# Third tokens loaded from ScalarE's queue instead of SyncE's, the third root on ScalarE, and the fourth statistics in two halves

## The chip, the cores and the metric

The kernel runs on one core of a Trainium2 chip. Its engines are TensorE (PE: matmuls, with its weight loads shown as PEld), VectorE (DVE), ScalarE (ACT), GpSimd (POOL) and SyncE (SP), which here only issues transfers. The metric is the device time of one execution in microseconds (us); lower is better. Beside it stands the span of the profiled execution, from its first to its last instruction.

## What is computed

Two mixers of the same input x (2048 tokens by 512 features) are blended by a gate. A is a spectral filter: a 2-D Fourier transform, a product with complex weights, the inverse transform. B normalizes each token, then runs a two-layer network over the token axis.

```python
def reference(A_x, A_w_r, A_w_i, B_x, B_w1, B_b1, B_w2, B_b2, gate_w):
    def _A_ref(x, w_r, w_i):
        X = rfft2(x.astype(float32), axes=(-2, -1))
        return irfft2(X * (w_r + 1j * w_i), s=(2048, 512), axes=(-2, -1)).astype(bfloat16)

    def _B_ref(x, w1, b1, w2, b2):
        h = _layernorm(x, axis=-1)                      # (x - mean) / sqrt(var + 1e-5)
        u = _gelu(einsum("bsd,sf->bdf", h, w1) + b1)    # S = 2048 -> F = 1792
        y = einsum("bdf,fs->bds", u, w2) + b2           # F -> S
        return y.transpose(0, 2, 1)

    x = A_x
    g = sigmoid((x * gate_w).sum(-1, keepdims=True))
    return g * _A_ref(x, A_w_r, A_w_i) + (1 - g) * _B_ref(x, B_w1, B_b1, B_w2, B_b2)
```

Both mixers take A_x; B_x is not read.

## The kernel before

The 2048 tokens are 16 blocks b of 128. The tokens of blocks 0 to 7 lie in the tile xa, those of 8 to 15 in xb; `hn` holds the normalized tokens. `w1a` holds the first 1024 of the 1792 columns of w1, by token block. The first long loop of TensorE (`mm1`, L279) goes over the token blocks: for each b it makes eight matmuls of 128x512, one for each group of 128 columns (ft), all eight adding up in PSUM over the 16 blocks. A block's matmuls need `hn` of that block and its part of `w1a`. Before the loop, L244 makes matmuls on a tile of zeros, and L243 turns the row b1 into a column with a matmul into a PSUM bank `pb`; ScalarE copies that to `bcol` (L305). The eighth column group of the loop takes over the bank of `pb`, so block 0's eighth matmul waits for that copy.

All order is written out by hand: engines run their instructions in the order of the program's text, and each waits by semaphores for what it needs. A wait stops its engine's later instructions too. A transfer of SP or ScalarE raises a semaphore when it has landed. There are eight such semaphores for both queues, taken in rotation; a transfer whose semaphore was used before waits until the earlier one has landed.

SP issues the loads at the start (L118 to L146): tokens of block 0, w1a of block 0, tokens 1, tokens 2, w1a 1, tokens 3, w1a 2, tokens 4 and 5, w1a 3 and so on. ScalarE issues b1 (`brow`, L121) in between.

The normalization of a block takes these steps:

- `bstat` (L250): statistics of the block's tokens, on VectorE; then their aggregate, `bn_aggr`, to mean and variance in `mv`.
- Blocks 0 and 1 (L300 to L307): ScalarE takes the square root (L303), VectorE the reciprocal (L306) and the normalization `norm_dve` (L275).
- Blocks 2 to 5: `aggr` (L255) adds 1e-5 on VectorE (L259) and takes the power -0.5 on GpSimd (L262); then `norm_dve`. The next block's statistics stand between, in the time in which GpSimd works.
- From block 6 on the normalization is an instruction of ScalarE (L271).

After the second root ScalarE loads the table for Sine (L309) and makes the angles `ma` and `mc` (L311, L312) for the Fourier tables.

Later TensorE alternates between the stages of the spectral filter, `token` (L513: L522, L525, L526), `dpass` (L534), `inv_tok` (L660, L666) and `inv_d` (L682), and products of the network that are pulled in between as filling (`fill`: L467 for the rest of the first layer, L477 and L809 for the second). Where each stage stands among the filling is fixed by the text (`fill_to`). VectorE prepares the stages' operands: YA and YB (L413 to L446), PMA and PMB (L540 to L571), then the outputs. L457 on ScalarE empties the second layer's banks, L811 on VectorE its last one.

Of the kernel before, what the change touches and what calls it, by code (L numbers as in the profile page):

```python
# [12 lines left out]
F32 = mybir.dt.float32  # L13
I32 = mybir.dt.int32

P = 128
# [6 lines left out]
NDVE = 6  # L23
# [20 lines left out]
def kernel(  # L44
# [13 lines left out]
    nc = tc.nc  # L58
# [5 lines left out]
    small = ctx.enter_context(tc.tile_pool(name="small", bufs=1))  # L64
# [3 lines left out]
    def H(i, shape, name, dt=BF16):  # L68
        return big.tile(shape, dt, tag=f"h{i}", name=name)
# [11 lines left out]
    xv = A_x[0].rearrange("(b a) d -> a b d", a=P)  # L81
    w1v = B_w1.rearrange("(b a) f -> a b f", a=P)
    w2v = B_w2.rearrange("(ft f) s -> f ft s", f=P)
    xh = [H(0, [P, 8, D], "xa"), H(1, [P, 8, D], "xb")]
# [4 lines left out]
    def load_x(b0, b1):  # L89
        nc.sync.dma_start(out=xh[b0 // 8][:, b0 % 8:(b1 - 1) % 8 + 1], in_=xv[:, b0:b1])  # L90

    def load_w1a(b0, b1):
        nc.sync.dma_start(out=w1a[b0 // 4][:, b0 % 4:(b1 - 1) % 4 + 1], in_=w1v[:, b0:b1, 0:FT1 * P])
# [27 lines left out]
    nc.scalar.dma_start(out=brow[:], in_=B_b1.rearrange("(ft f) -> ft f", f=P))  # L121
    load_w1a(0, 1)
    load_x(1, 2)
    for b in range(1, 3):
        load_x(b + 1, b + 2)
        load_w1a(b, b + 1)
    load_x(4, 6)
    load_w1a(3, 4)
    load_x(6, 8)
# [101 lines left out]
    stats = small.tile([P, NB, nc.vector.BN_STATS_DIM], F32, name="stats")  # L231
    mv = small.tile([P, NB, nc.vector.BN_AGGR_DIM], F32, name="mv")
# [16 lines left out]
    def bstat(b):  # L249
        nc.vector.bn_stats(out=stats[:, b, :], in_=xh[b // 8][:, b % 8, :])  # L250

    def on_dve(b):
        return b <= NDVE or b == NB - 2

    def aggr(b0, b1):  # L255
        for b in range(b0, b1):
            nc.vector.bn_aggr(out=mv[:, b, :], in_=stats[:, b, :])
        eng = nc.vector if on_dve(b0) else nc.gpsimd
        eng.tensor_scalar(mv[:, b0:b1, 1], mv[:, b0:b1, 1], 1e-5, 0.0, op0=Alu.add, op1=Alu.add)  # L259
        if not on_dve(b0):  # L260
            nc.gpsimd.tensor_scalar(nmr[:, b0:b1], mv[:, b0:b1, 0], -1.0, 0.0, op0=Alu.mult, op1=Alu.add)
        nc.gpsimd.tensor_tensor(rstd[:, b0:b1], mv[:, b0:b1, 1], c_mhalf.to_broadcast([P, b1 - b0]), op=Alu.pow)  # L262
# [11 lines left out]
    def norm_dve(b):  # L274
        nc.vector.tensor_scalar(hn[:, b, :], xh[0][:, b, :], mv[:, b, 0:1], rstd[:, b:b + 1],  # L275
                                op0=Alu.subtract, op1=Alu.mult)
# [20 lines left out]

    bcol = small.tile([P, NFT + NB], F32, name="bcol")
    b1f, b2f = bcol[:, 0:NFT], bcol[:, NFT:]
    for b in range(2):  # L300
        bstat(b)
        nc.vector.bn_aggr(out=mv[:, b, :], in_=stats[:, b, :])
        nc.scalar.activation(rstd[:, b:b + 1], mv[:, b, 1:2], ActF.Sqrt, bias=consts[:, 5:6], scale=1.0)  # L303
        if b == 0:
            nc.scalar.copy(b1f, pb[:, 0:NFT])  # L305
        nc.vector.reciprocal(rstd[:, b:b + 1], rstd[:, b:b + 1])  # L306
        norm_dve(b)  # L307
    bstat(2)
    nc.scalar.activation(sink[:], consts[:, 2:3], ActF.Sin, bias=c_mpi, scale=0.0)  # L309
    for v in range(2):  # L310
        nc.scalar.activation(ma[v][:], krow[:], ActF.Identity, bias=consts[:, 3 + v:4 + v], scale=acol[:, 0:1])  # L311
    nc.scalar.activation(mc[:], acol[:, 0:1], ActF.Identity, bias=consts[:, 4:5], scale=1024.0)  # L312


    aggr(2, 3)
    for b in range(2, NDVE):
        bstat(b + 1)
        norm_dve(b)
        aggr(b + 1, b + 2)
    bstat(NDVE + 1)  # L320
    norm(NDVE, NDVE + 1)
    aggr(NDVE + 1, NDVE + 2)
    norm(NDVE + 1, NDVE + 2)
    for b in range(NDVE + 2, NB, 2):
# [16 lines left out]
    for q in range(4):  # L341
        gprod(q)
        if q == 0:
# [10 lines left out]
                                in_=TD[:].rearrange("p s t k -> p (s t k)"))  # L354
    nc.sync.dma_start_transpose(out=TB[:].rearrange("p s t k -> p (s t) k"),
                                in_=TA[:].rearrange("p s t k -> p (s t k)"))
# [447 lines left out]
    b = NB - 1  # L804
# [36 lines left out]
```

## Time and profile before

| | |
|---|---|
| time, median of 3 runs | 128.1 us (127.78 to 128.22) |
| the profiled execution's own time | 128.74 us |
| its span | 127.0 us |
| mean granted TensorE clock | 0.998 |
| busy: TensorE, VectorE, ScalarE, GpSimd | 96%, 88%, 71%, 31% |
| HBM read, written | 19.15 MB, 3.67 MB |
| mean DMA rate | 189 GB/s (360 to 385 GB/s between 9.5 and 22 us) |

The busy share of an engine is a mean over the span. In the page's rows a group's time is followed by its mean for one instruction and by the idle time of its engine just ahead of it, with what ended that. In the order of time a row has the start, the time taken, the engine, the line, the operation, and what it writes and reads; SPq and ACTq are the issues of transfers on SP's and ScalarE's queues, whose time is that of the issue alone, not of the transfer. Matmuls overlap: one takes 0.38 us from start to end, but they follow each other every 0.216 us.

### The profile page before, as it was taken

How to read it: one execution, taken by the hardware profiler on the slowest of the kernel's cores; microseconds unless marked ns; L12 is line 12 of the kernel's file. 1: busy time of each engine (PE TensorE's matmuls, PEld its weight loads, DVE VectorE, ACT ScalarE, POOL GpSimd, SP SyncE). 2: the span in 40 equal slices, each digit the busy share in tenths (PEclk: the TensorE clock that was granted, in tenths of full speed). 3: DMA queues.
4: the chain of work that ended last, by engine and by line, in shares of the span. 5: the costliest groups of instructions: out<-in, count | busy, mean ns of one | idle time of the engine just before them, and what ended most of it. 6: DMA issues, size and time to landing. Idle time of an engine off the chain costs nothing.

```text
span 127.0 us, 2067 instructions
## 1 busy us (share of the span) xinstructions
PE 121.9 (96%) x737; PEld 65.3 (51%) x750; DVE 111.4 (88%) x190; ACT 89.6 (71%) x137; POOL 39.7 (31%) x71
## 2 busy tenths in 40 slices
PE   6999999999999999999999999999999999999990
PEld 2244444444444577657764775467644444444480
DVE  3799999999999999999999999999889999992140
ACT  4391379999799789998995699229795599422420
POOL 7133687998864595000050000000000000251200
PEclk9999999999999999999999999999999999999999
DMA  3899999998999999999979305810012101279991
GB/s 108 239 316 385 372 362 360 294 251 253 304 113 230 216 292 295 289 289 289 267 200 298 88 0 153 264 43 0 0 52 64 53 5 46 78 91 195 172 218 31
DMA packets 34699, 24.05 MB, mean 189 GB/s; under 512 B 5600, under 2 KB 32096, under 8 KB 34688
## 3 DMA queue, kind: packets, MB, share of 16 engines
q1 hardware_dynamic: 32580, 21.02, 63.2%
q0 software_dynamic: 1936, 2.76, 11.9%
q8 instruction: 6, 0.10, 0.3%
q10 hardware_dynamic: 172, 0.13, 0.3%
q14 instruction: 5, 0.04, 0.1%
HBM read 19.15 MB, written 3.67 MB: 180 GB/s over the span
## 4 chain that ended last, share of the span: by engine, by line
PE 93%; DMA 2%; DVE 1%; issue 1%; ACT 0%
PE yb L477 35%; PE u L279 23%; PE u L467 16%; PE ivt L666 5%; PE ivd L682 3%; PE dp L534 3%; PE yb L809 2%; PE tok L526 2%; PE tok L525 2%; DMA xa<-in_A_x_dram 2%; DVE stats L250 1%; PE ivt L660 0%; PE tok L522 0%; DVE hn L275 0%; DVE tbv L811 0%
## 5 line engine op out<-in xcount | busy, mean ns | idle before, releaser
L477 PE MATMUL yb<-gl,w2t 128*128 128x512 bf16 x203 | 46.4, 379 | 0.4
L477 PEld LDWEIGHTS <-w2t 128*128 128x128 bf16 x210 | 20.2, 98 | 22.0
L279 PE MATMUL u<-hn,w1a 128*128 128x512 bf16 x126 | 28.7, 388 | 0.2
L467 PE MATMUL u<-hn,w1b 128*128 128x512 bf16 x92 | 22.6, 379 | 0.2
L457 ACT ACTIVATE tbv<-yb,ombb,omg 128x512 bf16<-128x512 f32 x15 | 11.6, 776 | 15.8 <-PE yb L477 15.8
L279 PEld LDWEIGHTS <-w1a 128*128 128x128 bf16 x128 | 12.7, 99 | 16.2 <-issue 2.0
L787 POOL DMA_DIRECT2D out_dram<-ap x3 | 4.0, 1530 | 48.9 <-DVE ap L782 44.8
L467 PEld LDWEIGHTS <-w1b 128*128 128x128 bf16 x96 | 9.0, 98 | 8.0
L290 ACT ACTIVATE junk<-prod 128x512 bf16<-128x512 bf16 x16 | 10.1, 632 | 0.3
L361 ACT ACTIVATE gl<-u,bcol 128x512 bf16<-128x512 f32 x14 | 9.1, 685 | 1.0 <-PE u L279 0.8
L638 ACT CAST R<-ivt 128x1024 bf16<-128x1024 f32 x8 | 7.8, 1040 | 2.3 <-PE ivt L666 2.3
L262 POOL TENSOR_TENSOR rstd<-mv,consts 128x1 f32<-128x1 f32 (+1 forms) x10 | 6.5, 652 | 7.5 <-DVE mv L259 7.5
L638 ACT CAST H<-ivd 128x1024 bf16<-128x1024 f32 x7 | 6.9, 1050 | 0.8 <-PE ivd L682 0.8
L271 ACT ACTIVATE hn<-xb,nmr,rstd 128x512 bf16<-128x512 bf16 x8 | 5.8, 801 | 0.9 <-POOL nmr L266 0.9
L796 DVE TENSOR_TENSOR tbv<-tbv,ap 128x512 bf16<-128x512 bf16 x3 | 1.3, 426 | 5.8 <-ACT tbv L457 5.8
L250 DVE BATCH_NORM_STATS2 stats<-xa 128x6 f32<-128x512 bf16 x8 | 5.5, 686 | 0.6 <-DMA xa<-in_A_x_dram 0.5
L556 DVE TENSOR_TENSOR tatb<-PMA,wn 128x1024 bf16<-128x1024 bf16 x8 | 5.0, 688 | 0.2 <-PE tok L526 0.2
L606 POOL TENSOR_SCALAR omg<-g__765 128x16 f32<-128x16 f32 x1 | 0.7, 704 | 14.1 <-ACT g__765 L604 14.1
L682 PEld LDWEIGHTS <-R 128*128 128x128 bf16 x64 | 3.8, 98 | 2.5 <-ACT R L638 2.5
L250 DVE BATCH_NORM_STATS2 stats<-xb 128x6 f32<-128x512 bf16 x8 | 5.1, 674 | 0.0
L556 DVE TENSOR_TENSOR tatb<-PMB,wn 128x2048 bf16<-128x2048 bf16 x4 | 4.7, 1226 | 0.2
L527 ACT CAST ZA<-tok 128x1024 bf16<-128x1024 f32 x4 | 4.0, 1018 | 1.4 <-PE tok L526 1.3
(198 smaller groups left out, 226.5 us busy)
## 6 DMA issues: line engine op xcount, KB each, us to landing
w2t<-in_B_w_dram SPq DMA_DIRECT2D x8, 896.0 KB, 9.6
w1b<-in_B_w_dram SPq DMA_DIRECT2D x3, 1024.0 KB
w1a<-in_B_w_dram SPq DMA_DIRECT2D x8, 256.0 KB, 5.2
out_dram<-tbv SPq DMA_DIRECT2D x14, 128.0 KB, 4.4
out_dram<-ap POOLq DMA_DIRECT2D x3, 512.0 KB, 6.9
w1a<-in_B_w_dram SPq DMA_DIRECT2D x2, 512.0 KB
w1a<-in_B_w_dram SPq DMA_DIRECT2D x1, 1024.0 KB
xa<-in_A_x_dram SPq DMA_DIRECT2D x4, 128.0 KB, 3.2
```

What stands on the lines that cost most here:

```text
L250: nc.vector.bn_stats(out=stats[:, b, :], in_=xh[b // 8][:, b % 8, :])
L262: nc.gpsimd.tensor_tensor(rstd[:, b0:b1], mv[:, b0:b1, 1], c_mhalf.to_broadcast([P, b1 - b0]), op=Alu.pow)
L279: nc.tensor.matmul(u1[ft], lhsT=w1a[b // 4][:, b % 4, ft * P:(ft + 1) * P], rhs=hn[:, b, :], start=(b == 0), stop=(b == NB - 1))
L290: nc.scalar.activation(junk[:], prod[b // 8][:, b % 8], ActF.Copy, accum_out=glog[:, b:b + 1])
L361: nc.scalar.activation(gl[:, ft, :], src, ActF.Gelu_apprx_tanh, bias=b1f[:, ft:ft + 1], scale=1.0)
L457: nc.scalar.activation(tbv[0][:, b], y[:], ActF.Identity, bias=gate["ombb2"][:, b:b + 1], scale=gate["omg"][:, b:b + 1])
L467: nc.tensor.matmul(u[:], lhsT=w1b[c][:, b, k * P:(k + 1) * P], rhs=hn[:, b, :], start=(b == 0), stop=(b == NB - 1))
L477: nc.tensor.matmul(y[:], lhsT=w2t[b // 2][:, ft, (b % 2) * P:(b % 2 + 1) * P], rhs=gl[:, ft, :], start=(ft == 0), stop=(ft == NFT - 1))
L556: mul(tt[:, i, :, r:r + n], PM[:, 2 * s:2 * s + 2, r:r + n], w[:, None].to_broadcast([P, 2, n, 256]))
L638: nc.scalar.copy(out, pr[:].rearrange("p h n -> p (h n)"))
L666: nc.tensor.matmul(o[:, 2 * v:2 * v + 2], lhsT=UV[:, 2 * v + c, r, par::2], rhs=TB[:, s, c:c + 2], start=(c == 0), stop=(c == 1))
L682: nc.tensor.matmul(pr[:, c, o * P:(o + 1) * P], lhsT=plane(par, cos), rhs=TI[:, lst, t], start=True, stop=True)
```

## The change

The third tokens (block 2) are no longer issued by SP but by ScalarE, behind the root of block 0. On SP the second weights take their place, and what follows moves up by one. Block 2 goes the way of blocks 0 and 1: root on ScalarE, reciprocal on VectorE, instead of the addition on VectorE and the power on GpSimd. The statistics of block 3 are made in two instructions of 256 features each into a tile of their own, `st3`; the first stands between block 2's aggregate and its reciprocal, the second behind block 2's normalization. Both are aggregated together.

```diff
@@ -121,9 +121,9 @@
     nc.scalar.dma_start(out=brow[:], in_=B_b1.rearrange("(ft f) -> ft f", f=P))
     load_w1a(0, 1)
     load_x(1, 2)
-    for b in range(1, 3):
-        load_x(b + 1, b + 2)
-        load_w1a(b, b + 1)
+    load_w1a(1, 2)
+    load_x(3, 4)
+    load_w1a(2, 3)
     load_x(4, 6)
     load_w1a(3, 4)
     load_x(6, 8)
@@ -254,7 +254,7 @@
     def aggr(b0, b1):
         for b in range(b0, b1):
-            nc.vector.bn_aggr(out=mv[:, b, :], in_=stats[:, b, :])
+            nc.vector.bn_aggr(out=mv[:, b, :], in_=stats[:, b, :] if b != 3 else st3[:])
@@ -297,23 +297,31 @@
-    for b in range(2):
+    st3 = small.tile([P, 2, nc.vector.BN_STATS_DIM], F32, name="st3")
+
+    def bstat3(h):
+        nc.vector.bn_stats(out=st3[:, h, :], in_=xh[0][:, 3, 256 * h:256 * h + 256])
+
+    for b in range(3):
         bstat(b)
         nc.vector.bn_aggr(out=mv[:, b, :], in_=stats[:, b, :])
         nc.scalar.activation(rstd[:, b:b + 1], mv[:, b, 1:2], ActF.Sqrt, bias=consts[:, 5:6], scale=1.0)
         if b == 0:
+            nc.scalar.dma_start(out=xh[0][:, 2], in_=xv[:, 2])
             nc.scalar.copy(b1f, pb[:, 0:NFT])
+        if b == 2:
+            bstat3(0)
         nc.vector.reciprocal(rstd[:, b:b + 1], rstd[:, b:b + 1])
         norm_dve(b)
-    bstat(2)
     nc.scalar.activation(sink[:], consts[:, 2:3], ActF.Sin, bias=c_mpi, scale=0.0)
...
-    aggr(2, 3)
-    for b in range(2, NDVE):
+    bstat3(1)
+    aggr(3, 4)
+    for b in range(3, NDVE):
         bstat(b + 1)
         norm_dve(b)
         aggr(b + 1, b + 2)
```

## The prediction

> **What bounds the kernel now.** I read the page's busy shares, then the chain of waits, then the order of time at the start of the queues that the change touches. TensorE is busy for 96% of the span, and the chain that ended last is almost only TensorE:
>
> ```profile
> PE 121.9 (96%) x737; PEld 65.3 (51%) x750; DVE 111.4 (88%) x190; ACT 89.6 (71%) x137; POOL 39.7 (31%) x71
> ...
> PE 93%; DMA 2%; DVE 1%; issue 1%; ACT 0%
> ```
>
> The chain in order of time shows where TensorE is not yet the bound, namely before 4.90 us:
>
> ```profile
> 0.72 2.22 DMA xa<-in_A_x_dram
> 2.96 0.70 DVE stats L250
> ...
> 4.44 0.42 DVE hn L275
> 4.90 10.00 PE u L279 x41
> ```
>
> The first tokens land at 2.94, are normalized at 4.86, and from 4.90 on the matmuls of L279 follow each other. A row block b takes eight of them: at 0.43 us start to start up to 6.97 (the slow first stretch), 0.216 after that, so 1.73 us a block. The blocks start at 4.90, 7.62, 9.35, 11.07, 12.80. So nothing that arrives sooner than now, second weights or third tokens, can pull anything forward: TensorE has no wait there to lose. The change can gain only ahead of 4.90, and there it leaves tokens, weights and instructions as they are. It can lose, where hn of a block comes after its start.
>
> The cover that hn has is read on VectorE (start, duration):
>
> ```profile
> 4.76 0.68 DVE L250 BATCH_NORM_STATS2 stats<-xa 128x6 f32<-128x512 bf16 x1
> 5.48 0.18 DVE L302 BATCH_NORM_AGGREGATE mv<-stats 128x2 f32<-128x6 f32 x1
> 6.03 0.16 DVE L306 RECIPROCAL rstd<-rstd 128x1 f32<-128x1 f32 x1 [0.36 <-ACT rstd L303]
> 6.23 0.41 DVE L275 TENSOR_SCALAR hn<-xa,mv,rstd 128x512 bf16<-128x512 bf16 x1
> 6.56 0.68 DVE L250 BATCH_NORM_STATS2 stats<-xa 128x6 f32<-128x512 bf16 x1
> ```
>
> hn of block 1 is done at 6.64 (needed at 7.62), of block 2 at 8.76 (needed at 9.35), of block 3 at 10.12 (needed at 11.07). These covers, 0.6 to 1.0 us, are what the change spends.
>
> **The wait that comes with the moved transfer.** SP's queue, in order of time, and its waits:
>
> ```profile
> 2.60 0.43 SPq L93 DMA_DIRECT2D w1a<-in_B_w_dram  x1
> 3.08 0.43 SPq L90 DMA_DIRECT2D xa<-in_A_x_dram  x1
> 3.55 0.43 SPq L93 DMA_DIRECT2D w1a<-in_B_w_dram  x1
> ...
> 6.98 0.38 SPq L90 DMA_DIRECT2D xb<-in_A_x_dram  x1
> 7.40 0.56 SPq L93 DMA_DIRECT2D w1a<-in_B_w_dram  x1
> 8.40 0.38 SPq L90 DMA_DIRECT2D xb<-in_A_x_dram  x1
> ```
>
> ```profile
> SPq L90 <- DMA w1a<-in_B_w_dram: 1.0, 3, 0.4
> SPq L93 <- DMA xa<-in_A_x_dram: 0.9, 3, 0.3
> ```
>
> The first issues follow every 0.47 us; later ones stand and wait, loads of tokens on loads of weights and the reverse, though no data ties them. What ties them is a semaphore: the transfers that SP and ScalarE issue share eight in rotation, and each waits until the one before it on the same semaphore has landed. The issue at 6.98 stands behind the second weights (issued 2.60, landed 6.96), that at 7.40 behind the fourth tokens (3.08, landed 7.32), that at 8.40 behind the third weights (3.55, landed 8.38).
>
> In the built program of the changed kernel the moved load takes its place in that rotation too. Rows of ScalarE's and TensorE's order, with what each waits for:
>
> ```
> 5 L310 DMACopy xa<-in_A_x_dram 128x512 [waits DMAHW6_49]
> 6 L311 TensorCopy bcol<-pb 128x14 [waits PE_49]
> 7 L308 Activation rstd<-mv,consts 128x1 [waits DVE_49] x2
> 51 L279 Ldweights w1a [waits DMAHW6_49]
> ```
>
> Row 51 is block 2's first weight load, so semaphore 6 is that of the third weights: the third tokens are not issued at 4.2, behind the first root, but when the third weights have landed. ScalarE stands at that instruction, and behind it wait the copy of b1 (L311) and the roots of blocks 1 and 2.
>
> **The sum.** (1) Landing of the third weights. They are now issued in the place of the fourth tokens, 3.08. Bounds: 7.32, when what was issued at 3.08 lands now (128 KB less in total), and 8.38, their own landing now. Between: 7.85.
>
> (2) Root of block 1. The issue takes 0.43 (SP's xa) to 0.65 us (ScalarE's brow); with 0.43 it ends at 8.30. Then the copy, 0.17, the root, 0.29, and their gaps: 8.82. Reciprocal and normalization took 0.64 from the end of the root (6.00 to 6.64): hn of block 1 at 9.46, its matmuls at 9.52, not 7.62: 1.9 us late. (The eighth matmul of block 0 also waits, for the copy, whose bank it takes; it is ready at 8.55 and hides in this.) Eight matmuls end at 11.25.
>
> (3) Third tokens. Issued at 7.87. From issue to landing the loads of xa take:
>
> ```profile
> DMA to landing us min/median/max: 2.2/3.2/4.2
> ```
>
> The 2.2 is the first load, with idle queues; 4.2 is one with SP's backlog ahead of it, and SP's transfers of twice the size, issued near 5.5, take up to 5.6. I take the median, 3.2: this queue has nothing ahead of it, but the engines are full (busy share 0.93 or more from 5 to 12 us). Landed at 11.07, statistics at T = 11.09.
>
> The Trainium skill, "DMA: Bandwidth & Descriptors", section Queues, rings and completion order, says that each DMA engine goes round the queues packet by packet, so that a queue with little in it does not stand behind another's backlog. Estimated from that, one weight packet of eight rows (8 x 84 ns) goes ahead and it is 2.2 + 0.67 = 2.9, which makes the sum 0.3 smaller.
>
> (4) hn of block 2. From start of statistics to end of normalization block 1 took 6.64 - 4.76 = 1.87 with the same instructions (the third root is now also on ScalarE; the old way over POOL took 2.21). The first half of the fourth statistics now stands in the 0.36 us in which VectorE waited for the root. A half costs 0.34 (half of 0.68) to 0.68 (all fixed); I take 0.42, nearer the half because 512 elements at 0.68 leave little fixed, so 0.1 sticks out: T + 1.97 = 13.06. Matmuls at 13.12, not 9.35: 3.77 late.
>
> (5) hn of block 3: second half 0.42, aggregate and addition 0.41 with gaps, POOL's power 0.59 and 0.12 round it, normalization 0.41, less 0.09 by which VectorE starts one instruction ahead of the last one's end: T + 3.83 = 14.92, matmuls at 14.98, not 11.07: 3.9 late. Block 2 ended at 14.85, so this wait is 0.13.
>
> (6) After that VectorE needs 1.35 us a block (8.76 to 10.12) and TensorE 1.73, so no further wait. VectorE, busy without a gap over 0.2 us from here to 89, starts the fifth statistics at T + 2.63 = 13.72, not 9.05. That is 4.67 late, 0.77 more than TensorE. The closest places later: YA of L422 is done 1.37 before its weight load, PMA and PMB (L566) 1.15 and 1.13. All over 0.77, so nothing is added. ScalarE's Sine table, ma and mc (4.06 us) run from 12.3 to 16.4, before its hn of block 6 can start (13.93 + 4.67 = 18.6). Saved POOL and VectorE work (0.59; 0.15) lies off the path.
>
> (7) What else moves: SP issues everything from the second weights on 0.47 earlier, waits included; no reader waited for these, worth 0.
>
> Sum: +3.9 us. Span 127.0 to 130.9, this execution 128.74 to 132.6; the median 128.1 is 0.64 under the profiled one, so 132.0.
>
> **The clock.** TensorE would stand idle about 1.1 us (7.4 to 8.55), 0.8, then 1.9 (11.25 to 13.12), after it has reached 0.216 at 6.97. No row of before shows a pause of that kind after the slow stretch. The Trainium skill, "TensorE: Matmul & The Clock Gate", Part 1, says that a free-running window of about 3.4 us decides, and that an idle one halves the clock. In this trace the window that ends at 6.97 was 97% busy and ended the slow stretch, the one before it 75% busy and did not; what half-busy windows do in a fast stretch isn't shown.
>
> **Rivals.** A, the forecast. B, A with the slow spacing again: over 8 matmuls it costs 8 x 0.211 = 1.7 us; less if it falls into the waits (0.4), more if it lasts two blocks (3.4). Time 132.4 to 135.4, 133.7 in the middle. For it: half-busy stretches; against: both pauses are short.
>
> C, the other side: the issuing engine is not held, or the semaphore is free early. Then the load is issued at 4.22 and lands at 6.4 to 8.4, 7.4 in the middle; hn of block 3 at 7.45 + 3.83 = 11.28, 0.06 more to its matmul: TensorE 0.27 late, 128.4; with a landing before 7.1 nothing is late, VectorE and POOL are relieved, and 128.1 or a few tenths less remains. It decides if ScalarE's load starts before 7.1 minus 2.2 = 4.9. Against it: the three SP waits above, none of which began its issue before the landing.
>
> D, VectorE's lateness outgrows the later covers: if the half statistics cost 0.68 and the landing spreads, VectorE is 1.3 late against TensorE and the covers of 1.13 break: +0.2 on A. Inside A's range.
>
> **Numbers.** A (with D) 0.70, B 0.21, C 0.09. A's own range: landings 7.32 + 2.2 give T = 9.56 and +2.4 (130.5); 8.38 + 4.2 give T = 12.62 and +5.4 (133.5). The far end of the landing, 5.6, would give 134.9; with it and B in the upper tail the range is cut at 134.4, and at 130.4 below. A measurement here separates about 0.3%, 0.4 us: C is split into 0.06 within it, 0.02 faster, 0.01 slower; A and B are slower.
>
> **What would show it.** In the changed profile: ScalarE's queue issuing xa near 7.9 with the third weights as releaser; root of block 1 near 8.5, not 5.70; VectorE's third statistics near 11; TensorE's waits on hn of blocks 1 and 2, 1.9 us each, and none at L525 or L666. I am wrong if that issue stands at 4.2, if xa lands within 2.2 us, or if L279's spacing is 0.43 after 9 us.

## The result, and the profile after

The changed kernel takes 136.98 us (median of 6, 136.33 to 138.11), the kernel before 128.16 (median of 6, 127.78 to 128.75): the ratio is 1.0682, with a 95% interval of [1.065, 1.0714]. It is slower by 8.8 us. The forecast was 132.0 with a range of 130.4 to 134.4: the direction was right, the size too small by 5.0 us, and the measured time lies outside the range.

The profiled execution of the changed kernel took 136.74 us, with a span of 135.0 and a mean clock of 0.987 (before: 128.74, 127.0 and 0.998). First its page, with the busy shares and the chain of waits by engine:

```profile
PE 124.0 (92%) x750; PEld 65.4 (48%) x750; DVE 111.7 (83%) x191; ACT 90.0 (67%) x138; POOL 38.6 (29%) x70
...
PE 86%; DMA 8%; SPq 2%; DVE 1%; issue 0%; ACT 0%
```

TensorE's work is about the same (124.0 us, 121.9 before), in a span 8.0 longer; transfers have gone from 2% to 8% of the chain. The chain in order of time (start, duration) names them:

```profile
3.08 5.15 DMA w1a<-in_B_w_dram
8.25 5.38 DMA xa<-in_A_x_dram
13.65 0.70 DVE stats L250
14.38 0.19 DVE mv L307
14.60 0.30 ACT rstd L308
14.93 0.17 DVE rstd L314
15.13 0.42 DVE hn L275
15.59 25.98 PE u L279 x112
```

Before, the chain reached TensorE at 4.90. Now it runs through two transfers, one behind the other: the third weights (3.08 to 8.23), and then the third tokens, which ScalarE issues only when those have landed. From 15.59 on it is TensorE's again. So all the waiting lies ahead of the third block. ScalarE and its queue in order of time:

```profile
8.25 0.36 ACTq L310 DMA_DIRECT2D xa<-in_A_x_dram  x1
8.65 0.17 ACT L311 COPY bcol<-pb 128x14 f32<-128x14 f32 x1 [4.51 <-DMA w1a<-in_B_w_dram]
8.72 0.30 ACT L308 ACTIVATE rstd<-mv,consts 128x1 f32<-128x1 f32 x1
```

The moved load, placed behind the first root (which ends near 4.2), stands until 8.25. The copy of b1 and the second root stand behind it; the copy's bracket names the third weights as what ended a wait of 4.51 us. On TensorE, the bracket again being the idle time ahead of a row:

```profile
4.84 1.88 PE L279 MATMUL u<-hn,w1a 128*128 128x512 bf16 x7
8.88 0.38 PE L279 MATMUL u<-hn,w1a 128*128 128x512 bf16 x1 [2.15 <-ACT bcol L311]
9.72 1.89 PE L279 MATMUL u<-hn,w1a 128*128 128x512 bf16 x8 [0.46 <-DVE hn L275]
15.59 8.71 PE L279 MATMUL u<-hn,w1a 128*128 128x512 bf16 x32 [3.99 <-DVE hn L275]
```

Block 0's eighth matmul waits 2.15 for the copy, block 1 starts at 9.72 (7.62 before), block 2 at 15.59 (9.35 before). After that there is no pause. TensorE by stretches of 3.41 us, cut where the granted clock changes (columns: busy us and matmuls, granted clock, DMA share, GB/s):

```profile
5.30:8.71 3.41, 1.42 (x7) 1.00 0.88 286
8.71:12.13 3.42, 2.26 (x9) 1.00 1.06 385
12.13:15.54 3.41, 0.00 (x0) 1.00 1.08 365
15.54:18.95 3.41, 3.36 (x8) 0.50 1.04 356
```

In the third stretch TensorE does nothing; in the fourth its clock is halved (0.50), and block 2's eight matmuls take 3.37 us (15.59 to 18.96) instead of 1.73. Block 3 starts at 18.96, not 11.07: 7.9 us late, against 8.0 us more span.

### The profile page after: what moved, and what is told of

Read it like the earlier page. It is cut to its first block, busy times and chain, and to the rows that moved or that the text cites. A ratio compares the mean times of both kernels' runs of the same rounds, so it can differ in the third digit from the quotient of the medians.

```text
span 135.0 us, 2082 instructions
## 1 busy us (share of the span) xinstructions
PE 124.0 (92%) x750; PEld 65.4 (48%) x750; DVE 111.7 (83%) x191; ACT 90.0 (67%) x138; POOL 38.6 (29%) x70
## 4 chain that ended last, share of the span: by engine, by line
PE 86%; DMA 8%; SPq 2%; DVE 1%; issue 0%; ACT 0%
PE yb L485 34%; PE u L279 19%; PE u L475 15%; PE ivt L674 5%; DMA xa<-in_A_x_dram 4%; DMA w1a<-in_B_w_dram 4%; PE ivd L690 3%; PE dp L542 3%; PE yb L817 2%; PE tok L533 2%; PE tok L534 2%; SPq L90 1%; SPq L93 1%; DVE stats L250 1%; PE ivt L668 0%
## 5 line engine op out<-in xcount | busy, mean ns | idle before, releaser
L485 PE MATMUL yb<-gl,w2t 128*128 128x512 bf16 x210 | 47.4, 379 | 0.0
L279 PE MATMUL u<-hn,w1a 128*128 128x512 bf16 x128 | 30.1, 396 | 6.6 <-DVE hn L275 4.5
L475 PE MATMUL u<-hn,w1b 128*128 128x512 bf16 x96 | 23.3, 379 | 0.0
L262 POOL TENSOR_TENSOR rstd<-mv,consts 128x1 f32<-128x1 f32 (+1 forms) x9 | 6.0, 665 | 15.3 <-DVE mv L259 15.2
L250 DVE BATCH_NORM_STATS2 stats<-xa 128x6 f32<-128x512 bf16 x7 | 4.8, 687 | 4.5 <-DMA xa<-in_A_x_dram 4.5
L308 ACT ACTIVATE rstd<-mv,consts 128x1 f32<-128x1 f32 x3 | 0.9, 295 | 6.4 <-DVE mv L307 6.4
L690 PE MATMUL ivd<-TI,R 128*128 128x128 bf16 x64 | 4.9, 220 | 0.0
```

Source lines behind the costliest of these rows:

```text
L279: nc.tensor.matmul(u1[ft], lhsT=w1a[b // 4][:, b % 4, ft * P:(ft + 1) * P], rhs=hn[:, b, :], start=(b == 0), stop=(b == NB - 1))
L475: nc.tensor.matmul(u[:], lhsT=w1b[c][:, b, k * P:(k + 1) * P], rhs=hn[:, b, :], start=(b == 0), stop=(b == NB - 1))
L485: nc.tensor.matmul(y[:], lhsT=w2t[b // 2][:, ft, (b % 2) * P:(b % 2 + 1) * P], rhs=gl[:, ft, :], start=(ft == 0), stop=(ft == NFT - 1))
L690: nc.tensor.matmul(pr[:, c, o * P:(o + 1) * P], lhsT=plane(par, cos), rhs=TI[:, lst, t], start=True, stop=True)
```

## The experiments

Two questions were open: whether the moved transfer alone makes the loss or the rest of the change has a share, and why the transfer flew 5.38 us where the forecast had 3.2. Of the second there are two theories. "One line" (L in the expectations): a transfer lands only after all that any queue issued before it. "Own queue" (R): a queue with nothing ahead of it gets its turn at once, and lands in about the time that an idle queue needs.

### The rest of the change without the move, and the move alone

The first kernel puts the third tokens back on SP, and leaves the third root on ScalarE and the halved statistics (against the changed kernel):

```diff
-    load_w1a(1, 2)
-    load_x(3, 4)
-    load_w1a(2, 3)
+    for b in range(1, 3):
+        load_x(b + 1, b + 2)
+        load_w1a(b, b + 1)
...
-            nc.scalar.dma_start(out=xh[0][:, 2], in_=xv[:, 2])
```

> Third tokens back on SP in their old place; third root on ScalarE and fourth statistics in halves stay. Theory M (all of the loss comes from the moved transfer): nothing is held, block 2's hn comes about 0.2 us sooner than in the kernel before, TensorE has no wait to lose, time as before, 128.2 within 0.4 us. Theory N (the new root and the halves share in the loss, or help): under 127.7 or over 129.

The second has only the move and SP's order (against the kernel before):

```diff
-    for b in range(1, 3):
-        load_x(b + 1, b + 2)
-        load_w1a(b, b + 1)
+    load_w1a(1, 2)
+    load_x(3, 4)
+    load_w1a(2, 3)
...
+            nc.scalar.dma_start(out=xh[0][:, 2], in_=xv[:, 2])
```

> Only the transfer and SP's order changed; third root on GpSimd, fourth statistics whole. M: as the changed kernel, 137 (third tokens issued near 8.2, landed near 13.6; block 2 by the way over GpSimd 0.3 later, but the fourth statistics are then done sooner): 136.5 to 138. N: under 135.

Measured: without the move 128.13 against 128.21, 1.0013 [0.998, 1.0047]. With the move alone 137.75, 1.0729 [1.0689, 1.077]. The whole loss is the move's. TensorE without the move, in order of time:

```profile
4.80 25.49 PE L279 MATMUL u<-hn,w1a 128*128 128x512 bf16 x114
```

There is no pause from 4.80 on. hn of block 2 is done 0.43 us sooner than before (8.33, not 8.76), and that is worth nothing, since nobody waits for it. The chain of the move alone:

```profile
3.08 4.82 DMA w1a<-in_B_w_dram
7.92 6.61 DMA xa<-in_A_x_dram
14.55 0.70 DVE stats L250
15.73 0.59 POOL rstd L262
16.82 7.50 PE u L279 x25
```

It is the same two transfers, here with the second one 6.61 us long. From the statistics of block 2 to its first matmul it is 2.27 us here, by way of GpSimd (14.55 to 16.82), and 1.94 in the changed kernel (13.65 to 15.59): the new root saves 0.3 us where block 2's tokens decide. SP's queue in this run:

```profile
6.71 0.93 SPq L93 DMA_DIRECT2D w1a<-in_B_w_dram  x1
...
15.06 0.35 SPq L141 DMA_DIRECT2D brow<-in_B_b_dram  x1
```

The issue at 15.06 stands behind the landing (15.04) of the weights issued at 6.71. The moved load, issued 1.21 us after those weights, landed at 14.53, ahead of them. So "one line" isn't exact: a load can pass the one just ahead of it.

### The transfer behind the second root: does the hold of ScalarE matter?

```diff
         if b == 0:
-            nc.scalar.dma_start(out=xh[0][:, 2], in_=xv[:, 2])
             nc.scalar.copy(b1f, pb[:, 0:NFT])
+        if b == 1:
+            nc.scalar.dma_start(out=xh[0][:, 2], in_=xv[:, 2])
```

> Issue moved behind the root of block 1. Its semaphore is now that of the weights of block 3, landed at 9.5 in the changed kernel. If what counts is the landing of the third tokens: root 1 at 5.7 and block 1 in time at 7.6, issue near 9.5, landing near 14.9, block 2 near 16.8, and 1.2 us slower than the changed kernel: 138.2 (137.2 to 140 by the clock). If the hold of the root of block 1 counts: 2 us faster than the changed kernel, 135.

Measured: 137.96, 1.0775 [1.0716, 1.0834]. TensorE:

```profile
4.86 4.51 PE L279 MATMUL u<-hn,w1a 128*128 128x512 bf16 x16
17.66 12.70 PE L279 MATMUL u<-hn,w1a 128*128 128x512 bf16 x51 [8.29 <-DVE hn L275]
```

Blocks 0 and 1 run without a pause, so the copy and the second root are not held. The transfer, now behind that of the fourth weights in the rotation, is issued at 10.24 and lands 5.45 us later; the three waits have become one of 8.29. Holding the root and the copy costs nothing at the end: block 2's tokens decide.

### Zero matmuls in the gap: what the clock costs

Between blocks 1 and 2, sixteen matmuls add zeros to the sums (against the changed kernel):

```diff
+        if b == 1:
+            for n in range(16):
+                nc.tensor.matmul(u1[n % FT1].rearrange("p (n k) -> p n k", n=4), lhsT=warm[:],
+                                 rhs=warm[:, None, :].to_broadcast([P, 4, P]), start=False, stop=False)
```

> The changed kernel with 16 matmuls of zeros, added to the sums, between blocks 1 and 2: TensorE works from 11.6 to 15.0 where it was idle. If the idle window halved the clock: block 2 at 0.216 a matmul, 1.7 us less than the changed kernel, 135.2, and the spread of its runs (136.3 to 138.1) shrinks. If the slow spacing is no matter of idling: 137 or more.

Measured: 134.51 (134.29 to 134.97), 1.0494 [1.0464, 1.0525]. TensorE by stretches:

```profile
12.32:15.74 3.42, 2.44 (x12) 1.00 1.07 364
15.74:19.15 3.41, 3.36 (x16) 1.00 1.03 360
```

The clock stays at 1.00, and sixteen matmuls fit in a stretch where the changed kernel had eight. From the start of block 2 to the end of the span it is 117.4 us (15.15 to 132.6), in the changed kernel 119.4 (15.59 to 135.0). Of these 2.0 us, 1.64 are the eight slow matmuls; the rest isn't explained. The medians differ by 2.5, in which 0.4 is the earlier start of block 2 in this profile. They can differ by more than one halved stretch: the six runs of the changed kernel have mean clocks of 0.987 (three runs), 0.975 (two) and 0.962 (one), which are one, two and three halved stretches of 3.41 us in 135.

### The transfer issued early

Behind b1, ahead of everything else on ScalarE (first diff), or ahead of the first root (second):

```diff
     nc.scalar.dma_start(out=brow[:], in_=B_b1.rearrange("(ft f) -> ft f", f=P))
+    nc.scalar.dma_start(out=xh[0][:, 2], in_=xv[:, 2])
```

```diff
     nc.scalar.activation(sink[:], consts[:, 5:6], ActF.Sqrt, bias=consts[:, 5:6], scale=1.0)
+    nc.scalar.dma_start(out=xh[0][:, 2], in_=xv[:, 2])
```

> The third tokens on ScalarE's queue right behind b1, issued at 1.4, on a fresh semaphore. Theory L (one line: a transfer lands after everything that either queue issued before it): behind the first weights, landed near 4.3, first of all later ones. Theory R (each queue gets its turn): about the same. Both: nothing late, time as before, 128.2 within 0.4 us. If ScalarE's queue itself is slow: landed after 7, 129 or more.

> The third tokens on ScalarE's queue ahead of the first root, issued near 3.0, on a fresh semaphore, nothing held. L: behind what SP issued by then (fourth tokens, issued 2.6, landed 6.9), so landed near 7.3, 4.3 after the issue; hn of block 2 near 9.3, at its limit: 128.2 to 128.6. R: landed near 5.9, 2.9 after the issue; 128.2.

Measured: 128.44 against 128.40, 1.0000 [0.9981, 1.0019], and 128.46, 1.0011 [0.9991, 1.003]. Both are as fast as before. In the first:

```profile
1.41 0.36 ACTq L122 DMA_DIRECT2D xa<-in_A_x_dram  x1
...
6.57 0.68 DVE L251 BATCH_NORM_STATS2 stats<-xa 128x6 f32<-128x512 bf16 x1
```

The load is issued at 1.41, ahead of most of SP's, and VectorE comes to block 2's statistics at 6.57 without a wait. The second was expected to issue near 3.0; it issued at 1.48, beside the table load, so it repeats the first and does not tell the theories apart. Being on ScalarE's queue costs nothing; being late does.

### No hold, long line; no hold, short line

To take the hold away and leave the place behind the first root, SP's later loads were merged, so that the moved load's turn in the rotation falls on the semaphore of the second tokens, which land at 4.32:

```diff
-    load_x(4, 6)
+    load_x(4, 8)
     load_w1a(3, 4)
-    load_x(6, 8)
-    load_w1a(4, 5)
-    load_w1a(5, 6)
-    load_x(8, 10)
-    load_w1a(6, 7)
...
+    load_w1a(4, 6)
+    load_x(8, 12)
+    load_w1a(6, 8)
```

> The changed kernel with SP's later loads merged (tokens 4 to 7, weights 4 and 5, tokens 8 to 11, weights 6 and 7), so that the moved transfer's semaphore is that of the second tokens, landed at 4.7: issued near 4.7, root 1 not held. R: landed 2.9 to 3.2 after the issue, near 7.8; block 2 within 0.5 of its time; 128.2 to 128.8. L: behind all that SP issued by 4.7 (2.4 MB in all), landed near 11.5, 6.8 after the issue; block 2 near 13.5, 4.2 late, and 1.7 more if the clock drops: 132.4 to 134.2. If the semaphore was the whole cause: 128.2.

Measured: 134.12, 1.0436 [1.0392, 1.048]. SP's and ScalarE's queues and VectorE in order of time:

```profile
4.03 1.26 SPq L93 DMA_DIRECT2D w1a<-in_B_w_dram  x2
4.34 0.36 ACTq L306 DMA_DIRECT2D xa<-in_A_x_dram  x1
...
10.74 0.69 DVE L246 BATCH_NORM_STATS2 stats<-xa 128x6 f32<-128x512 bf16 x1 [4.15 <-DMA xa<-in_A_x_dram]
```

The load is issued at 4.34, when the second tokens have landed, with neither the copy nor the second root late, and is there 6.4 us later. It lands at 10.71, right behind the fourth weights (issued 4.03, landed 10.54) and ahead of the next (4.58, 12.08). That is one line; on its own queue it was expected 2.9 to 3.2 us after the issue, between 7.2 and 7.5. The merging itself put more ahead of the load: tokens 6 and 7, 256 KB, now belong to a transfer issued before it.

In the counterpart SP itself is held: a transfer of 512 bytes that waits for the mean of block 0 (and copies it to a scratch tile) stands ahead of SP's later loads, so that only those up to the third weights are ahead of the moved load:

```diff
-    load_x(4, 6)
-    load_w1a(3, 4)
...
+    scr = small.tile([P, 1], F32, name="scr")
+
+    def later_loads():
+        nc.sync.dma_start(out=scr[:], in_=mv[:, 0, 0:1])
+        load_x(4, 6)
+        load_w1a(3, 4)
...
             nc.scalar.dma_start(out=xh[0][:, 2], in_=xv[:, 2])
+            later_loads()
```

> The changed kernel, but a transfer of 512 bytes that waits for block 0's mean stands on SP's queue ahead of tokens 4 and 5, so that SP has issued no more than the third weights when ScalarE issues the third tokens at 4.2, and these get a free semaphore (that of b1). L: landed right behind the third weights, near 8.3; block 2 1.1 late, 1.2 in all, no idle window: 129.4 (129.0 to 129.8). R: landed 2.9 to 3.2 after the issue, near 7.3: 128.2 to 128.4. If the moved transfer is slow whatever stands ahead: landed near 9.6, 130.7.

Measured: 129.15 against 128.57, 1.0047 [1.0029, 1.0065].

```profile
3.94 0.36 ACTq L314 DMA_DIRECT2D xa<-in_A_x_dram  x1
...
7.46 0.69 DVE L254 BATCH_NORM_STATS2 stats<-xa 128x6 f32<-128x512 bf16 x1 [0.79 <-DMA xa<-in_A_x_dram]
```

Issued at 3.94, landed at 7.44, 3.5 us later, next behind the third weights (6.95). This time lies between the two expectations, and the run alone decides nothing. Beside the run above it does: two loads, issued 0.4 us apart on the same queue, one with 1,408 KB of SP's transfers issued and not landed, one with 640 KB (768 with the second tokens, which land 0.3 us after the issue), take 6.4 and 3.5 us. The difference of 640 to 768 KB over 2.9 us is 230 to 270 GB/s; all transfers together moved 315 and 281 GB/s during these two flights. In this run hn of block 2 is done at 9.35, within 0.05 us of the end of block 1, and block 3 waits 0.2 us; the rest of the 0.6 us by which it is slower isn't explained.

### A third queue, and smaller pieces

The load from GpSimd's queue, which is not in the rotation (placed behind its last table row, so that it is issued near 3.6):

```diff
+    nc.gpsimd.dma_start(out=xh[0][:, 2], in_=xv[:, 2])
...
-            nc.scalar.dma_start(out=xh[0][:, 2], in_=xv[:, 2])
```

> The third tokens from GpSimd's queue, behind its last iota (3.7), with a semaphore of its own kind; nothing on ScalarE is held. L, if the line takes in this queue too: landed behind what SP issued before about 4, so 8.2 to 9.6; block 2 1 to 2.3 us late: 129.2 to 130.6. If this queue gets its turn (R): landed near 6.9 and nothing late, 128.2 to 128.5.

Measured: 130.71 against 128.57, 1.019 [1.0139, 1.024]. Its chain:

```profile
3.60 5.29 DMA xa<-in_A_x_dram
8.92 0.70 DVE stats L251
10.86 1.89 PE u L280 x8
```

Issued at 3.60, it takes 5.29 us, and lands between the third weights (8.47) and the tokens that SP issued at 3.55 (9.15). Block 2 is 1.5 us late, and the clock stays at 1.00 in this run (one of the four, at 131.59 us, has a mean of 0.987). It lands where one line would have it, but for the tokens that SP issued 0.05 us before it. That GpSimd's queue is in the line is not shown by this alone: no run has a load from this queue with nothing ahead, so it could also be slow by itself.

SP's loads of tokens 4 to 9 and the weights between them in pieces of 128 KB, so that less stands ahead of the load:

```diff
-    load_x(4, 6)
-    load_w1a(3, 4)
...
+    load_x(4, 5)
+    half_w1a(3, 0)
+    half_w1a(3, 1)
+    load_x(5, 6)
...
```

> The changed kernel with SP's loads from tokens 4 to tokens 9 cut into pieces of 128 KB, so that the seven transfers that can stand on SP's queue hold 0.9 MB and not 1.8 MB. The moved transfer's semaphore is that of tokens 5, landed near 9.5. L: from issue to landing about half of 5.4, 2.7 us. If the engines' load alone makes it slow (R): 5.4 as before, since they are as full.

Measured: 135.41 (2 runs), 1.055 [1.0499, 1.0601]. The load, held on the semaphore of the tokens of block 5, is issued at 8.86 and lands 4.0 us later, between the two expectations. Loads issued at 8.32, 8.86 and 9.27 landed at 12.28, 12.86 and 13.22; the one that SP issued at 8.79, 0.07 us before the moved one, landed at 13.04, just behind it. Seven pieces of 128 KB and its own are 1.05 MB; at the 276 GB/s that all transfers moved during the flight that is 3.8 us. The engines' load alone, by which it would have been 5.4 as before, doesn't explain it. TensorE is busy for 1.05 us of the stretch from 7.58 to 11.00, and the next two stretches have half the clock.

## Why the prediction was wrong, and where it was right

**Steps 1 and 2 held.** The hold through the shared semaphore came as read from the built order: third weights at 8.23 (forecast 7.85, bounds 7.32 to 8.38), issue at 8.25 (7.87), second root at 8.72 (near 8.5), block 1's matmuls at 9.72 (forecast 9.52), the eighth matmul of block 0 at 8.88 (forecast 8.55). The late landing makes 0.38 us.

**Step 3 failed, the flight of the third tokens.** It took 3.2 us from issue to landing, because "this queue has nothing ahead of it". It was 5.38. The view that shows why is SP's queue of the changed kernel:

```profile
7.02 0.52 SPq L93 DMA_DIRECT2D w1a<-in_B_w_dram  x1
8.92 0.38 SPq L90 DMA_DIRECT2D xb<-in_A_x_dram  x1
...
12.35 0.34 SPq L140 DMA_DIRECT2D gwb<-in_gate_w_dram  x1
13.05 0.35 SPq L141 DMA_DIRECT2D brow<-in_B_b_dram  x1
13.65 0.39 SPq L93 DMA_DIRECT2D w1a<-in_B_w_dram  x1
```

The last three issues each begin as the earlier owner of their semaphore lands: tokens 8 and 9 (12.34), the weights issued at 7.02 (13.04), and the third tokens (13.63). The tokens issued at 8.92 land at 14.14. So the load from ScalarE, issued at 8.25, took its place between SP's issues of 7.02 and 8.92. The first of its packets moved only at 11.16. At 8.25, seven loads of 256 KB had been issued and not landed, 1.84 MB; with its own 0.13 it is 1.97 MB, and at the 365 to 385 GB/s of the stretches above that is 5.1 to 5.4 us. The forecast had all of this before it: the rate in its table of the profile before, SP's backlog, and the row of transfers behind that backlog, up to 5.6 us, which it put down as a far end and cut from the range. It took the median of loads that stood behind less.

The same working for every run that issues the load at 3.6 us or later, with the rate of its own flight:

| run | issued and not landed, with its own | GB/s of all transfers in the flight | quotient | measured |
|---|---|---|---|---|
| changed kernel | 1.97 MB | 374 | 5.3 us | 5.38 us |
| behind the second root | 1.97 MB | 372 | 5.3 us | 5.45 us |
| zero matmuls | 1.97 MB | 368 | 5.3 us | 5.82 us |
| move alone | 1.97 MB | 347 | 5.7 us | 6.61 us |
| small pieces | 1.05 MB | 276 | 3.8 us | 4.00 us |
| no hold, short line | 0.92 MB | 281 | 3.3 us | 3.50 us |
| GpSimd's queue | 1.44 MB | 276 | 5.2 us | 5.29 us |
| no hold, long line | 1.57 MB | 315 | 5.0 us | 6.37 us |

So the backlog at issue, not the queue, makes most of the flight. The quotient is always the smaller one, by 0.1 to 1.4 us; what the rest is isn't shown.

The Trainium skill, "DMA: Bandwidth & Descriptors", section Queues, rings and completion order, has each DMA engine go round the queues packet by packet. By it the forecast estimated 2.9 us; 5.38 was measured. Of the seven loads ahead of it the load passed at most the last: in the move alone, and with the zero matmuls (issued 7.36, landed 13.18, against 6.64 and 13.66). The same page's section Issuing engines are not separate DMA queues says that issuing from several engines saves only the time of issuing; the runs agree in that no kernel with the load on another queue was faster than the one before (128.44 against 128.40 at best).

**Steps 4 and 5 held, from a later T.** From the start of the statistics to hn took 1.89 us (13.65 to 15.54; forecast 1.97). VectorE in order of time:

```profile
13.65 0.69 DVE L250 BATCH_NORM_STATS2 stats<-xa 128x6 f32<-128x512 bf16 x1 [3.99 <-DMA xa<-in_A_x_dram]
14.38 0.18 DVE L307 BATCH_NORM_AGGREGATE mv<-stats 128x2 f32<-128x6 f32 x1
14.48 0.39 DVE L303 BATCH_NORM_STATS2 st<-xa 128x6 f32<-128x256 bf16 x1
14.93 0.16 DVE L314 RECIPROCAL rstd<-rstd 128x1 f32<-128x1 f32 x1
15.13 0.41 DVE L275 TENSOR_SCALAR hn<-xa,mv,rstd 128x512 bf16<-128x512 bf16 x1
```

The first half of the statistics costs 0.39, the second 0.42 (0.42 was estimated for each), and the first fills the time in which the root is made. hn of block 3 is done at 17.42; at full rate block 2 would have ended at 15.59 + 1.73 = 17.32, and the small wait of step 5 would have been there. With the halved clock it is hidden. The zero matmuls, with the clock at 1.00, show it:

```profile
15.78 0.68 DVE L250 BATCH_NORM_STATS2 stats<-xa 128x6 f32<-128x512 bf16 x1
16.57 0.41 DVE L275 TENSOR_SCALAR hn<-xa,mv,rstd 128x512 bf16<-128x512 bf16 x1
```

There hn of block 3 is done at 16.98, block 2 ends at 15.15 + 1.73 = 16.88, and block 3 starts at 17.04, a wait of 0.16 (forecast 0.13).

**Steps 6 and 7 held, but the changed kernel doesn't put step 6 to the test.** In it the fifth statistics start at 16.22, not 9.05, which is 7.17 late, less than TensorE's 7.89, since the halved clock gave VectorE time. With the zero matmuls they start at 15.78, 6.73 late, and block 3's matmuls are 5.97 late: 0.76 more for VectorE, where step 6 had 0.77, and TensorE has no wait on VectorE behind block 3. So the covers hold, and rival D did not come. The rest of the change is worth nothing where tokens come in time, 1.0013 [0.998, 1.0047].

**The clock** was worth nothing in the sum; it was put to rival B with 0.21, for half-busy stretches of short pauses. Its halving came, but behind the failure of step 3: with 5.38 us the pause ahead of block 2 grew to 3.99 and a whole stretch was empty. Its size was right: 3.37 - 1.73 = 1.64 us, where B had 1.7; B's time, 132.4 to 135.4, did not hold the measured one either, as it stood on A's flight. The Trainium skill, "TensorE: Matmul & The Clock Gate", Part 1, speaks of a free-running window of some 3.4 us whose idleness halves the clock; the trace agrees, with 0.50 granted from 15.54 on after 3.41 us without a matmul.

**The sum.** Span forecast 130.9, measured 135.0: 0.38 (weights) + 2.18 (flight) - 0.09 (normalization) + 1.64 (clock) - 0.13 (step 5's wait, hidden by the clock) = 3.98 of the 4.1. The rest of the 5.0 is the way from one execution to the median: the forecast took off 0.64, as before, but the median of the changed kernel lies 0.24 above the profiled run, where half of its runs have, by their mean clocks, more than one halved stretch.

**Rival C was priced wrongly as well.** It had 128.4 for an engine that isn't held. The merged kernel is that case, with 256 KB more ahead of the load, and it takes 134.1: 5.7 us are lost without a hold of the copy and the root, to the line and the halved clock behind it. Ranked by time lost, with what stands in the way of the load: hold, long line and clock, 8.8; no hold, long line and clock, 5.7; GpSimd's queue at 3.60, 2.1; no hold and a short line, 0.6; ahead of the line, 0.

None of the kernels beats the one before: where tokens come in time, TensorE runs without a pause from 4.9 us on, and there is nothing for earlier tokens to shorten. Left open is why the queues are served almost in one line, in the making of the transfers' descriptors or in the DMA engines; no run here tells these apart. Why the same 1.97 MB take 5.4 us in one kernel and 6.6 in another isn't explained either.

## What to carry to other kernels

Price a moved transfer by all that any queue has issued and not landed at that moment, divided by the rate of that stretch, and take that as the least: the flights here were 0.1 to 1.4 us longer. An empty queue of its own is no reason to take less. See in the built order which semaphore it gets, since on a computing engine its wait also holds what stands behind it. And if the pause that results approaches 3.4 us on TensorE, add the time of the matmuls that may then run at half the clock.

## What the runs showed of the hardware

- A load issued from ScalarE or GpSimd landed among SP's loads near its place in the order of issue: it passed at most the one issued just before it (in the move alone issued 1.21 us later and landed 0.5 us sooner, 7.92 to 14.53 against 6.71 to 15.04). The first packet of ScalarE's load moved 2.9 us (issue 8.25, packet 11.16) and 3.6 us (4.34, 7.95) after the issue behind a long line, and 2.0 us (3.94, 5.90) behind a short one.
- The clock was halved after stretches of 3.41 us with TensorE busy for up to 1.05 us (0.00, 0.54, 0.72, 1.05 in four kernels: up to 31%), and kept after 1.42, 1.55 and 2.26 (42, 45 and 66%). It came back after 2.71 us and more (79%), not after 2.55 (75%). Where between 31 and 42% the bound lies isn't shown.
- A transfer on ScalarE's queue that waits for nothing was issued at 1.48, while ScalarE's table load (1.41 to 2.69), which stands ahead of it in the program's text, was still running.
